# One planned TensorE stream of attention and feed-forward: new durations in the planner, new due times

## The chip, the cores and the metric

The kernel runs on one core of one Trainium2 chip. The metric is device microseconds of one execution. One more execution was recorded by the hardware profiler; all rows below come from it. The engines are TensorE (PE, with its weight loads as PEld), VectorE (DVE), ScalarE (ACT), GpSimd (POOL) and SyncE (SP), which issues the DMAs.

## The reference

Attention over 4 batches, 8 heads, 768 positions and head size 64, then a feed-forward network (FFN) over its 3072 tokens:

```
k_sum, v_sum = max of k, mean of v over blocks of 32 keys      # 24 of each
local  = q k^T / 8, only where |i - j| < 16
blocks = q k_sum^T / 8 + log(32)
a      = softmax over [local, blocks];  x = a @ [v, v_sum]      # 3072 x 512
out    = relu(x @ w_in)^2 @ w_out                               # 512 -> 2048 -> 512
```

## The kernel before, in words

**Tiling.** Attention works on 48 groups of 64 queries (12 to a batch), all 8 heads at once. For each group `softmax` masks and exponentiates (DVE L830, ACT L887) and normalises on DVE (L906) or, as a letter of `NORMAL_BY` says, on ACT (L913). `visit` multiplies with v for a pair of groups, and splits the 128 x 256 result x in two float32r parts, `xh` (ACT L1062) and `xl` (DVE L1065), from which the FFN reads. The block maxima of k come from `batch_k`: a DMA per head pair (`KL`), then DVE L566 (`KM`).

**Weights.** `w_in` and `w_out` are 16 items f each, converted by `convert` on ACT and DVE (L1131, L1137, L1145) into two float32r parts, which stay in SBUF.

**FFN.** Tokens are in 6 units of 512. Units 0 and 1 are plain: for each of 16 items f, `ffn` computes h = w_in^T x (task `FIu_f`, 12 matmuls, L1195), relu into `rl` (`RL`, ACT L1204), its square (`SQ`, L1205), a rounded copy `gh` (`GH`, L1206) and the rest `gl` (`GL`, DVE L1209), and then adds to the output in PSUM (`FOu_f`, L1219). There are two `h` tiles and one `rl` tile: `FI` of item f + 2 needs `RL` of item f done, and `RL` of item f + 1 needs `GL` of item f done. Items 0 and 1 of unit 0 run in halves of 256 tokens (`a`, `b`). `put` copies the outputs out of PSUM (L1256, `PC`) and stores them. Units 2 to 5 go as two couples through seven products of sums of blocks (`products`, `mixed`, L1514, L1731). For these `combine` (POOL L1300) and `combine_in` form sums of `w_out` and `w_in` for 8 pairs p of items, two halves each. `combine_in` adds the parts (`RCi`, L1364), sums blocks (`SCi`, L1379), and splits (ACT L1382, DVE L1385); a letter of `HALF_SUMS_BY` gives the sums of a pair to POOL or DVE. The result `ci` is stored to DRAM and read back later.

**What sets the order.** No instruction is placed by hand. Each piece of work is a `Task` with an engine, a modelled duration, a due time (`key`), tasks that it follows, and buffers that it takes or uses. `Plan.order()` simulates the five engines: whenever an engine is free it starts the ready task with the lowest due time whose buffers are free, and lets it last its modelled duration. The order of starts is the order in which the kernel's instructions are issued, one queue for each engine; at run time every engine works its queue strictly in that order and waits by semaphores. So a modelled duration costs the chip nothing: it only changes which task comes first. The due times are constants at the head of the file (`VISITS`: when each pair of groups is due; `SUMS`: each half of `combine_in`; `COMBS`: each `combine`; and so on). In the model a DVE task of a kind named in `SHARED`, started while POOL is busy, lasts longer by the factor `slows` of the POOL task times what it shares with it. Temporaries of 128 x 1024 float32 (weights in conversion, `cr`, `cs`, `ci`, output tiles `os`) take turns in three buffers `t`, in the order planned: a tile can start when the tile before it in its buffer is through, its store included.

Of the kernel before, what the change touches and what calls it, by code (L numbers as in the profile page):

```python
# [28 lines left out]
SQ = 32  # L29
# [25 lines left out]
FV_AT = 60.61, 233.96  # L55
# [130 lines left out]
class Plan:  # L186
# [26 lines left out]
    def order(self):  # L213
# [15 lines left out]
        for t in self.tasks:  # L229
# [3 lines left out]
            t.shared = t.engine == "DVE" and kind in self.SHARED  # L233
# [20 lines left out]
        while events:  # L254
# [25 lines left out]
            for e, tasks in ready.items():  # L280
# [46 lines left out]
def attention_then_relu2_ffn(  # L327
# [268 lines left out]
    def batch_v(b):  # L596
# [78 lines left out]
        if own:  # L675
# [4 lines left out]
            done(add(f"VM{b}", "PE", 1.4, sum_up, key + 8, [*all_loads, t_means], take=[out_ps], use=all_x))  # L680
# [92 lines left out]
    def window(g):  # L773
# [9 lines left out]
        return add(f"KW{g}", "ACT", 0.63, copy, wanted(g - 2) + 3, keys_of(g - 1, range(NPAIR))[1:], take=[x])  # L783
# [6 lines left out]
    def first_attention(g):  # L790
# [212 lines left out]
    def visit(both, then=(), block_sums=None):  # L1003
# [15 lines left out]
        if block_sums:  # L1019
# [6 lines left out]
            block_sums_done(add(f"VM{g}", "PE", 1.4, sum_up, due - 1, more, take=[out_ps], use=x))  # L1026
# [10 lines left out]
        def products():  # L1037
# [5 lines left out]
            f"V{both[-1]}" if n else f"S{then[0]}", "PE", 0.54 * n + 0.11 * (n == 1) + 0.49 * len(then), products, due, deps, take=take + [s] * bool(s), use=use,  # L1043
# [127 lines left out]
    def ffn(u, f, o, done, half=None):  # L1171
# [31 lines left out]
        t1 = t_FI[u, f] = add(f"FI{name}", "PE", 2.73 if half is None else 2.0, hidden, due, deps, take=[h], use=wi)  # L1203
        t2 = add(f"RL{name}", "ACT", act, lambda: nc.scalar.activation(cut(r), cut(h), AF.Relu), due + 3, [t1], take=[r], use=[h])  # L1204
# [782 lines left out]
```

## Time and profile before

| | us |
|---|---|
| median of 3 runs | 584.36 |
| lowest and highest run | 582.04, 586.36 |
| span of the profiled execution | 581.0 |
| TensorE busy in it | 563.0 (97%) |
| VectorE, ScalarE, GpSimd busy | 452.2, 373.7, 134.5 |

The profiled execution is known by its span alone: the lowest timed run is 1.04 us above it, the median 3.36, so what lies around the span is at least about that. Of the page's slices, TensorE shows 9 tenths in nearly all from the fourth on, with its clock at full speed; VectorE's busy share is highest in the first 16 of 40 slices (up to 230 us) and falls to half in the last third; the DMA engines are at 8 to 9 tenths up to slice 24 (350 us) and at 5 to 7 after it. The FFN's plain units and most of the attention lie before 300 us; the products of the two couples fill the rest. A row such as `[1.24 <-DMA scr_s<-cs]` says how long the engine stood idle before that instruction and which event ended it.

### The profile page before, as it was taken

The numbers are of one execution on the slowest core, as the hardware profiler recorded it, in microseconds if no ns is written. First come the engines' busy times: TensorE is split into PE (matmuls) and PEld (weight loads), VectorE is DVE, ScalarE is ACT, GpSimd is POOL, SyncE is SP. The second block draws the span as 40 slices with busy tenths as digits, with TensorE's granted clock in tenths as the row PEclk, the third lists the DMA queues.
The fourth block names the chain that finished last, engine by engine and source line by source line (L and its number), as shares of the span: only waits on it lengthen the run. The fifth ranks groups of instructions, "written<-read, shape, count | busy, mean of one in ns | idle before, by whom it ended". The sixth has DMA issues, their size and how long they took to land.

```text
span 581.0 us, 12047 instructions
## 1 busy us (share of the span) xinstructions
PE 563.0 (97%) x4052; PEld 460.2 (79%) x4052; DVE 452.2 (78%) x1015; ACT 373.7 (64%) x968; POOL 134.5 (23%) x193
## 2 busy tenths in 40 slices
PE   7879999999999899999999999999999999999997
PEld 6668787888887688887888888888888888888885
DVE  4899999685799997879976978869932656868864
ACT  1899899786757787768765768464634642454442
POOL 4300010167669469500043430000000000000000
PEclk9999999999999999999999999999999999999999
DMA  8899996989997999999988888866875566667672
GB/s 298 295 382 340 332 337 243 323 327 341 304 381 236 327 358 338 364 333 335 312 271 246 268 257 257 268 181 192 256 240 175 178 195 192 196 195 226 196 227 98
DMA packets 88082, 157.15 MB, mean 270 GB/s; under 512 B 9066, under 2 KB 30926, under 8 KB 88022
## 3 DMA queue, kind: packets, MB, share of 16 engines
q1 hardware_dynamic: 88022, 156.39, 82.2%
q8 instruction: 32, 0.52, 0.4%
q14 instruction: 28, 0.23, 0.1%
HBM read 111.30 MB, written 44.66 MB: 268 GB/s over the span
## 4 chain that ended last, share of the span: by engine, by line
PE 76%; DVE 9%; DMA 8%; SPq 3%; issue 2%; ACT 1%; DVEq 0%; ACTq 0%
PE o L1514 23%; PE o L1731 14%; PE h L1195 9%; PE o L1219 9%; PE sz L1731 8%; PE att L1514 4%; PE x L997 3%; DMA raw<-wW 3%; PE att L756 2%; PE sa L1731 2%; PE att L1731 2%; DMA v<-vS 1%; DMA fv_lent<-vS 1%; DMA out<-os 1%; DVE ci L1379 1%
## 5 line engine op out<-in xcount | busy, mean ns | idle before, releaser
L1496 ACT CAST gh<-g 128x512 fp32r<-128x512 f32 x112 | 69.3, 621 | 63.2 <-DVE gl L1501 30.5
L1514 PE MATMUL o<-gh,w 128*128 128x512 f32 x384 | 103.0, 390 | 0.0
L1501 DVE TENSOR_TENSOR gl<-g,gh 128x512 fp32r<-128x512 f32 x112 | 76.8, 693 | 22.9 <-ACT gh L1496 22.4
L1514 PEld LDWEIGHTS o<-gh,w 128*128 128x128 f32 x384 | 71.8, 188 | 15.0
L1195 PE MATMUL h<-xh,w 128*128 128x512 f32 x240 | 76.2, 399 | 3.9 <-ACT rl L1204 3.9
L1768 ACT ACTIVATE g<-g 128x512 f32<-128x512 f32 x60 | 37.6, 630 | 49.5 <-DVE g L1764 49.3
L887 ACT ACTIVATE p<-p,small 128x118 f32<-128x118 f32 x160 | 61.1, 387 | 1.6 <-DVE small L830 1.6
L1219 PE MATMUL o<-w,gh 128*128 128x512 f32 x240 | 61.9, 394 | 0.0
L1514 PE MATMUL o<-gl,w 128*128 128x512 f32 x192 | 59.2, 389 | 0.0
L1195 PEld LDWEIGHTS h<-xh,w 128*128 128x128 f32 x240 | 45.1, 191 | 14.2 <-ACT rl L1204 4.7
L1219 PEld LDWEIGHTS o<-w,gh 128*128 128x128 f32 x240 | 44.4, 188 | 9.7 <-issue 0.4
L1195 PE MATMUL h<-xl,w 128*128 128x512 f32 x120 | 47.2, 394 | 0.0
L1514 PEld LDWEIGHTS o<-gl,w 128*128 128x128 f32 x192 | 36.0, 188 | 7.6
L1731 PE MATMUL o<-w,w 128*128 128x512 f32 x160 | 40.6, 390 | 0.0
L769 POOL COPY kb<-kb 128x96 f32<-128x96 f32 x25 | 10.9, 435 | 107.1 <-PE att L756 36.4
L1774 POOL TENSOR_TENSOR g<-g 128x512 f32<-128x512 f32 x16 | 22.6, 1418 | 53.7 <-ACT g L1768 53.1
L1731 PEld LDWEIGHTS o<-w,w 128*128 128x128 f32 x160 | 30.0, 188 | 6.3
L1491 DVE TENSOR_TENSOR g<-g 128x512 f32<-128x512 f32 x48 | 33.9, 716 | 1.2 <-POOL g L1774 0.7
L830 DVE CUSTOM_DVE_ANT_0 p<-att,mask 128x118 f32<-128x118 f32 x152 | 32.5, 272 | 2.6 <-PE att L756 2.6
L1731 PE MATMUL sz<-xh,w 128*128 128x512 f32 x128 | 34.5, 391 | 0.0
L1219 PE MATMUL o<-w,gl 128*128 128x512 f32 x120 | 33.6, 389 | 0.0
L1764 DVE CUSTOM_DVE_ANT_0 g<-sz,g 128x512 f32<-128x512 f32 x32 | 21.9, 685 | 13.2 <-ACT g L1751 6.4
(201 smaller groups left out, 1186.7 us busy)
## 6 DMA issues: line engine op xcount, KB each, us to landing
raw<-wW SPq DMA_DIRECT2D x32, 512.0 KB
w<-scr_t SPq DMA_DIRECT2D x64, 256.0 KB
w<-scr_s SPq DMA_DIRECT2D x64, 256.0 KB
w<-scr_a SPq DMA_DIRECT2D x48, 256.0 KB
w<-scr_i SPq DMA_DIRECT2D x44, 256.0 KB
turn<-a SPq DMA_DIRECT2D x18, 512.0 KB
scr_t<-ci SPq DMA_DIRECT2D x16, 512.0 KB
v<-vS SPq DMA_DIRECT2D x34, 192.0 KB
```

The lines of the kernel that those rows point to most:

```text
L830: nc.vector.tensor_tensor_reduce(out=pr.tile[:, j, :KEYS], in0=score_at(g, 0, j), in1=mask_of(g)[0], scale=-SCALE, scalar=-NEG, op0=ALU.ad ...
L887: nc.scalar.activation(x, score_tile(g, p % parts)[:, p] if by_pe else x, AF.Exp, bias=nm.tile[:, p : p + 1], scale=SCALE if by_pe else -1 ...
L1195: nc.tensor.matmul(cut(h), lhsT=lhs.tile[:, k // 2, k % 2 * P : (k % 2 + 1) * P], rhs=rhs[:, k, c0 : c0 + n], start=(i == 0), stop=(i == 3 ...
L1219: nc.tensor.matmul(o_of(o, t).rearrange("p (h c) -> p h c", h=2), lhsT=terms[i][0].tile[:, (t - t0) * P : (t - t0 + 1) * P], rhs=terms[i][ ...
L1491: lambda x=x, ins=ins, op=op: nc.vector.tensor_tensor(out=x.tile, in0=ins[0].tile, in1=ins[1].tile, op=op),
L1496: f"GH{s}_{n}", "ACT", 0.54, lambda x=x, gh=gh: nc.scalar.copy(out=gh.tile, in_=x.tile), due - GH_LEAD, ready,
L1501: lambda x=x, gh=gh, gl=gl: nc.vector.tensor_tensor(out=gl.tile, in0=x.tile, in1=gh.tile.bitcast(F32), op=ALU.subtract),
L1514: nc.tensor.matmul(o.tile[:, d], lhsT=chunk.tile[:, w * HALF + d * P : w * HALF + (d + 1) * P], rhs=y.tile, start=begins and w == 0 and y ...
L1731: nc.tensor.matmul(o.tile, lhsT=lhs(w, k), rhs=y[k], start=begins and i == 0, stop=i == 5, skip_group_check=not begins,)
L1764: lambda: nc.vector._custom_dve(TENSOR_ADD_SAT, out=to.tile, in0=o.tile, in1=x.tile, s0=HUGE, s1=0.0), key, deps,
L1768: f"G{name}_{s}", "ACT", 0.63, lambda: nc.scalar.activation(to.tile, to.tile, AF.Square), key + 0.7, [t], use=[to]
L1774: f"{name}_{s}", engine, cost, lambda: tensor.tensor_tensor(out=to.tile, in0=a.tile, in1=b.tile, op=ALU.subtract), key, deps,
```

## The change

It changes what the planner believes, and the due times; the tasks are the same, but that one group's normalisation moves from DVE to ACT (one letter of `NORMAL_BY`). Modelled durations become shorter for most small tasks (L1256 and others 0.69 to 0.615, half an `FI` 2.0 to 1.47, scores 1.1 to 0.97). The cost of a switch of TensorE to narrow tasks goes from 0.3 to 0.09, with 0.13 for the way back. `t.shared`, true or false before, becomes a factor: 2.5 for `SCi`, 1.5 for `N`, 1.8 for `XPL`, 1.2 for `RCi`, 1 for the other shared kinds. The due times are set anew, most of them by under 8 us.

```diff
+VM0_AT = -60
-FIRST_LS = -180
+FIRST_LS = -160
...
-NORMAL_BY = "DDDDDDDDDDDDAADDDDDAADDADDAAAADDADDDDAADAAAAAAAA"
...
+NORMAL_BY = 'DDDDDDDDDDDDAADDDDDAADDADDAAAADDADADDAADAAAAAAAA'
...
-COMBS = 113.9, 126.8, 141.39, 159.1, 177.9, 210.24, 223.15, 214.82
...
+COMBS = (113.677, 126.8, 141.39, 159.1, 178.36, 210.24, 219.634, 214.224)
...
-R_LEAD = 9
-TR_LEAD = 16.82
...
-X_LEAD = 5.36
...
+R_LEAD = 12
+TR_LEAD = 9.85
...
+X_LEAD = 18.99
...
-    SWITCH, NEAR = 0.3, 9.0
+    SWITCH, BACK, NEAR = 0.09, 0.13, 9.0
     NARROW = ("S", "V", "VM")
-    SHARED = "GL", "TA", "TB", "WJ", "WW", "SL", "SLi", "XD", "XSL", "XPL", "XW", "RCi", "SCi", "N"
+    SHARED = "GL", "TA", "TB", "WJ", "WW", "SL", "SLi", "XD", "XSL", "XPL", "XW", "XPL", "RCi", "SCi", "N"
+    TWICE = dict(SCi=2.5, N=1.5, XPL=1.8, RCi=1.2)
...
-            t.shared = t.engine == "DVE" and kind in self.SHARED
+            t.shared = self.TWICE.get(kind, 1.0) * (t.engine == "DVE" and kind in self.SHARED)
...
-                        cost += slows * min(cost, free["POOL"] - now)
+                        cost += slows * t.shared * min(cost, free["POOL"] - now)
                 if e == "POOL":
                     slows = t.slows
-                free[e] = end = now + cost + self.SWITCH * (t.narrow and not narrow)
+                if e == "PE":
+                    cost += self.SWITCH * (t.narrow and not narrow) + self.BACK * (narrow and not t.narrow)
+                free[e] = end = now + cost
...
-    SUMS = 121.7, 129.74, 148.43, 166.33, 195.88, 201.13, 197.53, 197.25, 153.98, 169.96, 168.64, 165.29, 173.06, 198.45, 180.64, 190.85
...
+    SUMS = (121.7, 122.391, 148.43, 166.33, 197.9, 203.15, 204.48, 196.35, 156.0, 171.98, 168.64, 166.253, 173.06, 198.338, 180.64, 190.85)
...
-    A0, A1, B0, B1 = 12.0, 2.0, 21.0, 2.2
-    HALF_AT = 26.97, 32.0
+    T0, SLOW, STEP = 28.0, 6.4, 6.68
+    MIXED_STEP = (1.54, 1.47)
+    X_BY = (20.008, 15.505)
+    SUMS = (121.7, 122.391, 148.43, 166.33, 197.9, 203.15, 204.48, 196.35, 156.0, 171.98, 168.64, 166.253, 173.06, 198.338, 180.64, 190.85)
+    PRODUCT_STEP = (1.517, 1.34)
+    A0, A1, B0, B1 = 10.3, 1.69, 21.18, 1.77
+    HALF_AT = (26.97, 32.657)
...
-        t1 = t_FI[u, f] = add(f"FI{name}", "PE", 2.73 if half is None else 2.0, hidden, due, deps, take=[h], use=wi)
-        t2 = add(f"RL{name}", "ACT", act, lambda: nc.scalar.activation(cut(r), cut(h), AF.Relu), due + 3, [t1], take=[r], use=[h])
-        t3 = add(f"SQ{name}", "ACT", act, lambda: nc.scalar.activation(cut(r), cut(r), AF.Square), due + 4, [t2], use=[r])
+        t1 = t_FI[u, f] = add(f"FI{name}", "PE", 2.72 if half is None else 1.47, hidden, due, deps, take=[h], use=wi)
+        t2 = add(f"RL{name}", "ACT", act - 0.04, lambda: nc.scalar.activation(cut(r), cut(h), AF.Relu), due + 3, [t1], take=[r], use=[h])
+        t3 = add(f"SQ{name}", "ACT", act - 0.02, lambda: nc.scalar.activation(cut(r), cut(r), AF.Square), due + 4, [t2], use=[r])
```

Line numbers of the changed kernel are 1 higher from line 40 on, 2 from line 198 on and 4 from line 314 on.

**VectorE before the first halves of the FFN (about 35 to 42 us).** An `xl_75` is the rest of one group's x, the last of them that of group 7, which `FI0_0b` needs; `raw`, `t` and `w` are weights in conversion; `p0` and `small3` with L899, L900 and L906 the normalisation of group 8. Before:

```order
L1131 TENSOR_SCALAR raw1_1_486<-raw1_1_486 128x512
L1065 TENSOR_TENSOR xl_75<-att1_69,xh_74 128x4x64
L1137 SCALAR_TENSOR_TENSOR t1_1_663<-t1_1_663,raw1_1_486 128x512
L1145 TENSOR_TENSOR w1_0_711<-t1_0_660,w1_0_711 128x2x256
L1131 TENSOR_SCALAR raw0_2_492<-raw0_2_492 128x512
L1131 TENSOR_SCALAR raw3_516<-raw3_516 128x1024
L899 TENSOR_SCALAR small3_88<-small3_88 128x4
L900 RECIPROCAL small3_88<-small3_88 128x4
L1145 TENSOR_TENSOR w1_1_730<-t1_1_663,w1_1_730 128x2x256
L1065 TENSOR_TENSOR xl_75<-att0_68,xh_74 128x4x64
L906 TENSOR_TENSOR p0_82<-p0_82,small3_88 128x4x118
L1065 TENSOR_TENSOR xl_75<-att1_69,xh_74 128x4x64
```

And with the change, `gl0_0a` being the first `gl` of the FFN:

```order
L1149 TENSOR_TENSOR w1_0_713<-t1_0_679,w1_0_713 128x2x256
L1141 SCALAR_TENSOR_TENSOR t1_1_739<-t1_1_739,raw1_1_490 128x512
L1069 TENSOR_TENSOR xl_75<-att1_69,xh_74 128x4x64
L1135 TENSOR_SCALAR raw0_2_501<-raw0_2_501 128x512
L903 TENSOR_SCALAR small3_88<-small3_88 128x4
L904 RECIPROCAL small3_88<-small3_88 128x4
...
L910 TENSOR_TENSOR p0_82<-p0_82,small3_88 128x4x118
L1149 TENSOR_TENSOR w1_1_753<-t1_1_739,w1_1_753 128x2x256
L1213 TENSOR_TENSOR gl0_0a_780<-rl0_0a_751,gh0_0a_777 128x256
```

Two L1131 (of `raw0_2` and `raw3`), the normalisation of group 8 and the last step of `w1_1` (L1145) stood ahead of the last `xl`; they now stand behind it (`raw3` further on). The work ahead of `gl0_0a` is nearly the same.

**VectorE in the middle (about 160 to 180 us).** `ci4_0` is the first half of the sums of `w_in` pair 4, `kb` the block maxima of a new batch, `gl1_2` to `gl1_4` the FFN's unit 1. Before:

```order
L1385 TENSOR_TENSOR ci1_0_2113<-ci1_0_2113 128x4x128
L1209 TENSOR_TENSOR gl1_2_2245<-rl1_2_2207,gh1_2_2238 128x512
L566 TENSOR_REDUCE kb_73<-kb_73 128x24 x3
L1209 TENSOR_TENSOR gl1_3_2280<-rl1_3_2248,gh1_3_2277 128x512
L1364 TENSOR_TENSOR ci4_0_2286<-w8_1133 128x2x128
L1364 TENSOR_TENSOR ci4_0_2286<-w9_1179 128x2x128
L1379 TENSOR_TENSOR ci4_0_2286<-ci4_0_2286 128x128 x4
L1385 TENSOR_TENSOR ci4_0_2286<-ci4_0_2286 128x4x128
L1209 TENSOR_TENSOR gl1_4_2353<-rl1_4_2288,gh1_4_2351 128x512
```

And with the change:

```order
L1213 TENSOR_TENSOR gl1_2_2236<-rl1_2_2176,gh1_2_2214 128x512
L1368 TENSOR_TENSOR ci4_0_2242<-w8_1174 128x2x128
L1368 TENSOR_TENSOR ci4_0_2242<-w9_1332 128x2x128
L1383 TENSOR_TENSOR ci4_0_2242<-ci4_0_2242 128x128 x4
L570 TENSOR_REDUCE kb_73<-kb_73 128x24 x2
L1389 TENSOR_TENSOR ci1_0_2234<-ci1_0_2234 128x4x128
L1213 TENSOR_TENSOR gl1_3_2303<-rl1_3_2244,gh1_3_2277 128x512
L1389 TENSOR_TENSOR ci4_0_2242<-ci4_0_2242 128x4x128
L1213 TENSOR_TENSOR gl1_4_2353<-rl1_4_2311,gh1_4_2350 128x512
```

The sums of `ci4_0` (two L1364, four L1379) stood behind `gl1_3`; they now stand ahead of two `kb`, of `ci1_0` and of `gl1_3`.

**ScalarE ahead of the relu of item 6 (about 176 to 185 us).** `xh` is the split of a pair's x, `kw29` the keys of group 29, `p0` and `p1` softmax of groups 26 and 27. Before:

```order
L1382 CAST ci5_1_2355<-ci5_1_2355 128x4x128
L1205 ACTIVATE rl1_5_2373<-rl1_5_2373 128x512
L1206 CAST gh1_5_2450<-rl1_5_2373 128x512
L1382 CAST ci1_1_2420<-ci1_1_2420 128x4x128
L1204 ACTIVATE rl1_6_2505<-h1_6_2404 128x512
L1062 CAST xh_74<-x23_2461 128x4x128
L1205 ACTIVATE rl1_6_2505<-rl1_6_2505 128x512
```

And with the change:

```order
L1210 CAST gh1_5_2467<-rl1_5_2355 128x512
L1386 CAST ci5_1_2357<-ci5_1_2357 128x4x128
L1066 CAST xh_74<-x23_2433 128x4x128
L891 ACTIVATE p0_82,small3_88<-p0_82,small3_88 128x118 x2
L1386 CAST ci1_1_2385<-ci1_1_2385 128x4x128
L891 ACTIVATE p0_82,small3_88<-p0_82,small3_88 128x118 x2
L891 ACTIVATE p1_83,small1_72<-p1_83,small1_72 128x118 x4
L917 ACTIVATE p0_82<-p0_82,small3_88 128x118 x4
L784 COPY kw29_2562<-kb_73 128x4x24
L785 COPY kw29_2562<-kb_73 128x4x94
L917 ACTIVATE p1_83<-p1_83,small1_72 128x118 x4
L1386 CAST ci5_0_2503<-ci5_0_2503 128x4x128
L1208 ACTIVATE rl1_6_2586<-h1_6_2401 128x512
L1209 ACTIVATE rl1_6_2586<-rl1_6_2586 128x512
```

The relu of item 6 stood ahead of the split for pair 23, of the keys and of two groups' exponentials and normalisations, and now stands behind them.

## Rows read from the trace of the kernel before

**Rows 1.** The page: its head, and busy time of the engines.
```profile
span 581.0 us, 12047 instructions
...
PE 563.0 (97%) x4052; PEld 460.2 (79%) x4052; DVE 452.2 (78%) x1015; ACT 373.7 (64%) x968; POOL 134.5 (23%) x193
```

**Rows 2.** Waits of TensorE: us in total, times, longest us.
```profile
PE h L1195 <- ACT rl L1204: 3.9, 3, 2.7
...
PE o L1731 <- DVE g L1764: 0.3, 1, 0.3
```

**Rows 3.** TensorE's timeline: start us, us, instruction, idle before it with releaser.
```profile
41.03 0.50 PE L1195 MATMUL h_0b<-xh,w 128*128 128x256 f32 x2 [1.65 <-ACT xh L1062]
...
69.79 0.73 PE L1195 MATMUL h<-xh,w 128*128 128x512 f32 x2 [0.81 <-ACT rl L1204]
```

**Rows 4.** VectorE's timeline before 42 us.
```profile
27.86 0.44 DVE L1131 TENSOR_SCALAR raw<-raw 128x512 uint32<-128x512 uint32 x1 [1.01 <-DMA raw<-wW]
...
38.67 1.02 DVE L1131 TENSOR_SCALAR raw<-raw 128x512 uint32<-128x512 uint32 x2
...
41.44 0.41 DVE L1065 TENSOR_TENSOR xl<-att,xh 128x256 fp32r<-128x256 f32 x1
```

**Rows 5.** TensorE's timeline at 201 us.
```profile
201.23 1.22 PE L1195 MATMUL h<-xh,w 128*128 128x512 f32 x2 [2.72 <-ACT rl L1204]
```

**Rows 6.** The chain of waits in order of time: start us, us, what.
```profile
201.23 4.55 PE h L1195 x12
...
208.51 2.72 PE h L1195 x12
```

**Rows 7.** Stretches: PE, PEld, DVE, ACT, POOL busy, PEclk, DMA share, GB/s.
```profile
42.00:44.00 2.00, 1.99 (x15) 1.79 (x16) 2.00 (x10) 2.00 (x5) 0.00 (x0) 1.00 1.03 327
...
180.00:190.00 10.00, 9.63 (x97) 7.76 (x95) 9.64 (x28) 5.97 (x21) 9.77 (x13) 1.00 0.60 206
...
200.00:205.00 5.00, 3.77 (x10) 3.02 (x11) 5.00 (x23) 4.89 (x16) 2.87 (x4) 0.66 1.07 382
...
210.00:215.00 5.00, 5.00 (x54) 3.91 (x54) 4.74 (x8) 2.61 (x5) 3.51 (x5) 1.00 1.06 411
```

**Rows 8.** VectorE's timeline from 157 to 200 us.
```profile
157.66 0.69 DVE L1256 COPY os<-o 128x512 f32<-128x512 f32 x1 [1.24 <-DMA scr_s<-cs]
...
161.66 0.68 DVE L1209 TENSOR_TENSOR gl<-rl,gh 128x512 fp32r<-128x512 f32 x1
...
162.26 2.67 DVE L566 TENSOR_REDUCE kb<-kb 128x24 f32<-128x768 f32 x3
...
166.50 1.78 DVE L1364 TENSOR_TENSOR ci<-w 128x256 f32<-128x256 f32 x2 [0.53 <-DMA out<-os]
...
168.31 2.92 DVE L1379 TENSOR_TENSOR ci<-ci 128x128 f32<-128x128 f32 x4
...
196.08 1.01 DVE L1379 TENSOR_TENSOR ci<-ci 128x128 f32<-128x128 f32 x4
...
197.64 0.71 DVE L1364 TENSOR_TENSOR ci<-w 128x256 f32<-128x256 f32 x2
...
199.81 0.68 DVE L1209 TENSOR_TENSOR gl<-rl,gh 128x512 fp32r<-128x512 f32 x1
```

**Rows 9.** GpSimd's timeline.
```profile
164.12 1.30 POOL L1300 TENSOR_TENSOR cr<-w 128x512 f32<-128x512 f32 x1 [7.24 <-PE o L1219]
```

**Rows 10.** The chain of waits: two landings.
```profile
160.64 5.74 DMA out<-os
...
256.12 4.87 DMA kb<-kT
```

**Rows 11.** ScalarE's timeline.
```profile
166.01 0.60 ACT L1204 ACTIVATE rl<-h 128x512 f32<-128x512 f32 x1 [0.36 <-DVE gl L1209]
...
184.64 0.60 ACT L1204 ACTIVATE rl<-h 128x512 f32<-128x512 f32 x1 [3.95 <-DVE gl L1209]
```

**Rows 12.** TensorE's timeline at 169 us.
```profile
169.41 0.63 PE L756 MATMUL att<-kb,q 64*64 64x118 f32 x16
```

More of the change, by code (lines that the diff above doesn't have):

```diff
@@ L654, in batch_v @@
             last = add(
-                f"VM{b}_{i}", "PE", 0.9, mm, key + i, loads + [t_means, last],
+                f"VM{b}_{i}", "PE", 0.98, mm, VM0_AT + i, loads + [t_means, last],
                 take=[out_ps] if i == 0 else [], use=[x] + [out_ps] * (i > 0),
@@ L781, in copy @@
             nc.scalar.copy(out=x.tile[:, :, NB:], in_=kb[:, :, k0 + NB : k0 + KEYS])
-        return add(f"KW{g}", "ACT", 0.63, copy, wanted(g - 2) + 3, keys_of(g - 1, range(NPAIR))[1:], take=[x])
+        return add(f"KW{g}", "ACT", 0.59, copy, wanted(g - 2) + 3, keys_of(g - 1, range(NPAIR))[1:], take=[x])
     def keys_of(g, pairs):
@@ L1024, in sum_up @@
                     mm()
-            block_sums_done(add(f"VM{g}", "PE", 1.4, sum_up, due - 1, more, take=[out_ps], use=x))
+            block_sums_done(add(f"VM{g}", "PE", 1.44, sum_up, due - 1, more, take=[out_ps], use=x))
         if then:
@@ L1042, in visit @@
         t_v = add(
-            f"V{both[-1]}" if n else f"S{then[0]}", "PE", 0.54 * n + 0.11 * (n == 1) + 0.49 * len(then), products, due, deps, take=take + [s] * bool(s), use=use,
+            f"V{both[-1]}" if n else f"S{then[0]}", "PE", 0.535 * n + 0.08 * (n == 1) + 0.485 * len(then), products, due, deps, take=take + [s] * bool(s), use=use,
         )
@@ L1534, in products @@
                 made["U1"] = add(
-                    f"U1_{s}", "ACT", 0.97, lambda o=o: nc.scalar.copy(out=by_two(u2), in_=o.tile), due, [t_p], take=[u2], use=[o]
+                    f"U1_{s}", "ACT", 0.92, lambda o=o: nc.scalar.copy(out=by_two(u2), in_=o.tile), due, [t_p], take=[u2], use=[o]
                 )
@@ L1603, in split @@
             t1 = add(
-                f"XSH{s}_{i}_{k}", "ACT", 0.62, lambda: nc.scalar.copy(out=hi[k].tile, in_=temps[i][k].tile), due + key,
+                f"XSH{s}_{i}_{k}", "ACT", 0.53, lambda: nc.scalar.copy(out=hi[k].tile, in_=temps[i][k].tile), due + key,
                 [*t_x[i, k], *needs, *t_X[s][at][:1], *(x_readers[0][at] if s else [])], take=take, use=[both[i]] + [hi[k]] * (not take),
@@ L1622, in sum_x @@
                 t = add(
-                    f"XW{s}_{i}_{k}", "DVE", 0.69, whole, due - XS_LEAD + i + 0.1 * k, [t_XL[g] for g in range(u * UG, (u + 1) * UG)],
+                    f"XW{s}_{i}_{k}", "DVE", 0.615, whole, due - XS_LEAD + i + 0.1 * k, [t_XL[g] for g in range(u * UG, (u + 1) * UG)],
                     take=[] if k else [both[i]], use=[both[i]] * k, behind=t if k else None, keeps=not k, begin=due - XS_LEAD - 4,
@@ L1634, in plainly @@
             t1 = add(
-                f"XPH{s}_{i}_{k}", "ACT", 0.62, lambda: nc.scalar.copy(out=hi, in_=temps[i][k].tile), due + key - 2, [*t_x[i, k], *deps],
+                f"XPH{s}_{i}_{k}", "ACT", 0.53, lambda: nc.scalar.copy(out=hi, in_=temps[i][k].tile), due + key - 2, [*t_x[i, k], *deps],
                 use=[both[i]],
@@ L1750, in evacuate @@
             return add(
-                f"{name}_{s}", "ACT", 0.59, lambda: nc.scalar.copy(out=to.tile, in_=o.tile), key, deps, take=take, use=[o] + [to] * (not take)
+                f"{name}_{s}", "ACT", 0.52, lambda: nc.scalar.copy(out=to.tile, in_=o.tile), key, deps, take=take, use=[o] + [to] * (not take)
             )
@@ L1755, in plus @@
             return add(
-                f"{name}_{s}", "DVE", 0.69, lambda: nc.vector.tensor_tensor(out=to.tile, in0=o.tile, in1=x.tile, op=ALU.add), key, deps,
+                f"{name}_{s}", "DVE", 0.615, lambda: nc.vector.tensor_tensor(out=to.tile, in0=o.tile, in1=x.tile, op=ALU.add), key, deps,
                 use=[o, x, to],
@@ L1831, in step @@
                         t = add(
-                            f"R21_{p}_{s}", "ACT", 0.6, lambda: nc.scalar.activation(second.tile, x.tile, AF.Relu), key, [t],
+                            f"R21_{p}_{s}", "ACT", 0.52, lambda: nc.scalar.activation(second.tile, x.tile, AF.Relu), key, [t],
                             use=[second, x],
@@ L1835, in step @@
                         t_G[s, p, 1] = add(
[L1836 removed]
+                            f"G21_{p}_{s}", "ACT", 0.57, lambda: nc.scalar.activation(second.tile, second.tile, AF.Square), key + 0.7,
                             [t], use=[second],
```

57 lines of the change are left out of this document (26 added, 31 removed).

## The prediction, before the changed kernel was run

> **What bounds the kernel now.** I read the page first: TensorE is busy 563.0 of 581.0 us [rows 1], so all that an order of work can win are 18.0 us, the start and the end of the program among them. No other engine is near that. The table of TensorE's waits comes next: where does it wait after the start? The relu is the releaser with the largest sum for the hidden products, 3.9 us in three waits, the longest 2.7 [rows 2]. So I went to TensorE's timeline for the places. There are two stretches.
>
> At the front, `FI0_0b`, the second half of the first hidden product, waits 1.65 us at 41.03, and `FI0_6` waits 0.81 for a relu at 69.79 [rows 3]. The first row names ScalarE's `xh`; VectorE's timeline shows the last `xl` at 41.44 [rows 4], so the splits of x as a whole are late there, and VectorE makes the last of them.
>
> In the middle, `FI1_9` waits 2.72 us at 201.23 [rows 5]. The chain of waits shows that this costs twice: its twelve matmuls take 4.55 us, where the next twelve take 2.72 [rows 6]. The stretch of 200 to 205 us has a mean granted clock of 0.66, so TensorE was for a part at 1.2 instead of 2.4 GHz [rows 7]. The loss is 4.55 − 2.72 = 1.83 us beside the 2.72 of the wait. After the wait of 1.65 us at 41.03 the granted clock was 1.00 [rows 3, 7]: a wait of that length cost no clock there.
>
> What is late at 201.23? The relu of item 8 needs the one `rl` tile back, and `gl1_7` on VectorE gives it at 199.81 + 0.68 [rows 8]. From 157 us on VectorE hardly stands still, so the sum of its work before `gl1_7` is what sets the time of that wait.
>
> **The change part by part.** The modelled durations, the switch costs and the factors cost the chip nothing: they only choose the order. TensorE, VectorE, ScalarE and GpSimd do the same work but for one normalisation that goes from VectorE to ScalarE after the two stretches; I cost it at nothing, since neither engine has TensorE waiting on it there, and if that cover went it would cost one VectorE instruction, below 1 us.
>
> *Front.* Between the start of the two L1131 at 38.67 and the last `xl` at 41.44 there are 2.77 us; less one other `xl` (0.41, as the row at 41.44) it is 2.36 us of work that now stands behind the last split [rows 4]. That is more than the 1.65 us which TensorE waited, so this wait should go. Against it, `gl0_0a`, which the next products need, keeps nearly its place; VectorE's idle time of 1.01 us at 27.86 [rows 4], before a weight that is waited for, can be filled by the new order and would bring `gl0_0a` forward by as much. So the gain lies between 0 and 1.65; I take 1.2, between the 1.01 that VectorE can give and the whole. The wait of 0.81 at 69.79 goes if two pieces of other TensorE work come between, as the new order of TensorE has it (the fourth output product and a visit): between 0 and 0.81, taken 0.8. Front: **2.0**, bounds 0 and 2.46.
>
> *Middle.* Three changes move `gl1_7`. (a) VectorE's idle 1.24 us at 157.66, before an output copy that waited for a buffer [rows 8], goes, since this copy now follows other work: 1.24 earlier. (b) The sums of `ci4_0` stood at 166.50 to 171.2, beside GpSimd, which is at work from 164.12 on after 7.24 us idle [rows 9]. They took 1.78 + 2.92 us there; the same two groups take 0.71 and 1.01 at 197.64 and 196.08 [rows 8]. Moved ahead, they save between 0 (beside GpSimd again) and 2.98 us. I take 1.7: `gl1_2` starts at 161.66 [rows 8], so that the sums come up to 3 us before GpSimd's start, but (c) they need a buffer whose output tile must first be stored. Before, such a store went from 160.64 for 5.74 us to 166.38 [rows 10], and the sums stood 0.53 waiting for it [rows 8]. In the new order the tile in question is an earlier one. The wait lies between 0 and 166.38 − 162.3 = 4.1; I take 1.9, rather below the middle because its stores now go out ahead of two loads of keys. So `gl1_7` comes 1.24 + 1.7 − 1.9 = 1.0 us earlier. The wait at 201.23 shrinks from 2.72 to 1.7, which is nearest to the row at 41.03 (1.65, no clock lost), so the 1.83 stay as well. Middle: 1.0 + 1.83 = **2.8**, bounds 0 and 2.72 + 1.83 = 4.55.
>
> *ScalarE's queue.* The relu of item 6 now stands behind a split, keys, eight exponentials and two normalisations. I cost this at nothing because ScalarE stood idle 3.95 us before it, waiting for VectorE [rows 11]: the work fits where the engine was idle. If that cover is gone, each us that the relu comes later is one of wait for `FI1_8`.
>
> *The queue of SyncE.* Stores and loads change places, among them the two loads of keys named above; what this may cost is the second rival. The rest of the program, from 300 us on, has VectorE at half load, and I found no wait of TensorE there that the new order touches.
>
> Sum: 2.0 + 2.8 = 4.8 us, so the span goes from 581.0 to 576.2. The profiled execution lies 3.36 us below the median and 1.04 below the fastest run; I take the saving off the median: 584.36 − 4.8 = **579.6**. One per cent is 5.8 us here, about what a measurement of this kernel tells from no change: faster begins below 578.5, slower above 590.2.
>
> **The rivals.**
>
> *B: the middle's gain is taken back by the DMA.* From 200 to 205 us the DMA engines are busy at a share of 1.07; room is only before, 10 × (1 − 0.60) = 4.0 us from 180 to 190 [rows 7]. The keys of the last batch land at 256.12 + 4.87 = 261.0 [rows 10], and their maxima let a sum start for which TensorE waits 0.3 us [rows 2]: there is no slack. If that landing stays where it is, a TensorE that arrives there 2.8 us sooner waits 2.8 us more. For it: no transfer up to there becomes smaller. Against it: the 4.0 us can be filled when the issues come sooner. Time: 584.36 − 2.0 = 582.4. A rule speaks for this rival: the Trainium skill, "SBUF — State Buffer", section "A bandwidth-pool intuition that's wrong (but worth ruling out)", gives HBM to one core some 358 GB/s and says that HBM is almost always the bottleneck. Here 382 GB/s were moved from 200 to 205 us and 411 from 210 to 215 [rows 7], above that figure, so the trace bears out that the stretch is full but not where the limit lies.
>
> *C: everything goes.* The three waits on a relu (3.9 [rows 2], with the 0.81 and the 2.72 among them), the 1.65 and the 1.83: 7.4 us, 577.0. For it: (c) is short if the store lands early, and then (b) gives its 2.98; `gl1_7` comes 4.2 earlier. Against it: the 1.9 above.
>
> *D: slower, by the buffer of `ci4_0`.* If the sums are held as long as before, to 166.4, VectorE stands idle from about 161.1 (162.3 less the 1.24) and then runs them beside GpSimd all the same: 166.4 + 4.70 = 171.1. Behind them wait two of the block maxima (2 × 0.89), one split (0.7) and `gl1_3` (0.7 [rows 8]), which ends near 174.3 instead of 166.0. The relu of item 4, which waited 0.36 for it at 166.01 [rows 11], ends near 174.9, and the visit that starts at 169.41 [rows 12] needs its `h` tile: TensorE waits 5.5 us and loses the clock (1.83, as at 201.23). It decides from the point where `gl1_3` is 169.41 − 166.6 = 2.8 us late; from there each us costs one. What comes back: the visit's delay takes up most of the wait at 201.23 and its clock, 3.9 of 4.55. With the front's 2.0 this gives 5.5 + 1.83 − 3.9 − 2.0 = 1.4 us more: 585.8, and beyond 590.2 where a second relu is late behind it, another 2.72 + 1.83 at item 6. For it: the buffers are three, and the landing of 5.74 us is in the trace. Against it: another tile's store, issued sooner.
>
> *E: the change doesn't do what it says.* The new order is different in places that TensorE doesn't feel: 584.4.
>
> **How the numbers follow.** The forecast has 0.47; its own range is 577 to 582, from the bounds of front and middle, and 0.4 of it lie below 578.5. B has 0.15, C 0.19, D 0.14 (half of it beyond 590.2), E 0.05. Faster: 0.47 × 0.4 + 0.19 = 0.38. Slower: 0.07. Within: 0.55. The range reaches from 575.0, two us under C, to 587.0, a little over the first case of D; what is left out is D's dearer half and a tail of C, about 0.1.
>
> **What would show it.** In the profile after: no wait of 1.65 us at `FI0_0b`, and VectorE's last `xl` near 39 us; no wait before the seventh item's hidden product; the `ci4_0` sums at 0.7 and 1.0 us rather than 1.78 and 2.92, with the idle time before them naming the store; the wait of `FI1_9` under 2 us with the clock at 1.00. I am wrong if the sums are again near 4.7 us, if another relu than item 8's stops TensorE between 165 and 200 us, or if the wait at the last keys grows beyond 0.3.

## The result, and the profile after

The change made the kernel slower. Beside the kernel before on the same chip its median was 587.74 us against 584.36 (7 runs each), a ratio of 1.0055 (95% interval 1.0034 to 1.0075); in a later series it was 586.81 against 584.62, 1.0039 (1.0008 to 1.0069). Both intervals lie above 1: the loss is small, but clear of noise. The forecast was 579.6, with a range of 575.0 to 587.0.

The profiled execution has a span of 586.0 us, 5.0 more than before [rows 1]; the medians lie 3.4 us apart, and a second profile of the changed kernel has a span of 582.1. What follows is read from the first one. The page's head and busy times:

```profile
span 586.0 us, 12045 instructions
...
PE 564.3 (96%) x4052; PEld 461.6 (79%) x4052; DVE 455.2 (78%) x1014; ACT 376.3 (64%) x972; POOL 133.2 (23%) x193
```

TensorE is busy 1.3 us longer, so 3.7 of the 5.0 us are idle. The table of TensorE's waits (us in total, times, longest) shows that the place that leads it is new:

```profile
PE o L1735 <- ACT os L1260: 4.1, 1, 4.1
```

Here are these places on TensorE's timeline (start, us, instruction, idle before it with its releaser). They answer to [rows 3, 5, 12]:

```profile
40.27 0.50 PE L1199 MATMUL h_0b<-xh,w 128*128 128x256 f32 x2 [0.27 <-ACT rl_0a L1208]
...
43.13 0.50 PE L1199 MATMUL h_1b<-xh,w 128*128 128x256 f32 x2 [1.18 <-ACT rl_1a L1208]
...
171.59 1.15 PE L1001 MATMUL x<-a,v 118*64 118x64 f32 x32 [1.70 <-ACT rl L1208]
...
201.12 1.22 PE L1199 MATMUL h<-xh,w 128*128 128x512 f32 x2 [2.08 <-ACT rl L1208]
...
261.52 1.48 PE L1735 MATMUL o<-xh,w 128*128 128x512 f32 x4 [4.13 <-ACT os L1260]
```

The wait of 1.65 us at `FI0_0b` is gone (0.27 left), and 1.18 stands in its place at `FI0_1b`. The visit at 171.6 waits 1.70 us, which it didn't before. `FI1_9` waits 2.08 instead of 2.72. And at 261.52 the sum `SP0_2` waits 4.13; before the change it began without a wait:

```profile
257.53 1.20 PE L1731 MATMUL o<-xh,w 128*128 128x512 f32 x4
```

If one sets the end of each TensorE task beside its end before, the course of the whole is seen: 0.24 us ahead at 50 us (`FI0_2`), 1.03 ahead at 81 (`FO0_5`), 0.65 ahead at 169 (`FO1_1`), 1.18 behind at 176 (`FO1_2`), 0.18 ahead again at 257 (`VM3`), 5.63 behind at 267.5 (`SP0_4`) and 4.78 behind at the end. So in this pair of executions the loss, 4.98 us from 0.18 ahead to 4.80 behind, arises between 257 and 301 us: 4.13 of wait and 1.7 of clock behind it (8 us at 0.79, where it was 1.00 before), less 0.8 that comes back, 0.29 of it the wait that the kernel before has at 263.55. The stretches (columns as in [rows 7]), two of the changed kernel and then one of the kernel before:

```profile
200.00:205.00 5.00, 3.88 (x11) 3.07 (x12) 5.00 (x22) 4.75 (x17) 3.85 (x6) 0.66 1.03 340
...
262.00:270.00 8.00, 8.00 (x30) 6.38 (x29) 6.58 (x10) 3.99 (x10) 0.00 (x0) 0.79 1.01 366
```

```profile
262.00:270.00 8.00, 7.71 (x88) 5.69 (x86) 8.00 (x15) 6.44 (x14) 0.27 (x1) 1.00 1.05 380
```

At 201 us the clock falls as before (0.66 in both [rows 7]).

What ended the wait at 261.52 is read from VectorE's timeline, from SyncE's and from the chain of waits. VectorE first:

```profile
254.47 0.64 DVE L910 TENSOR_TENSOR p<-p,small 128x472 f32<-128x472 f32 x1
258.96 0.69 DVE L1260 COPY os<-o 128x512 f32<-128x512 f32 x1 [3.85 <-DMA scr_s<-cr]
...
260.20 0.65 DVE L1260 COPY os<-o 128x512 f32<-128x512 f32 x1
```

`SP0_2` needs the PSUM tile that the last two of unit 1's four output copies empty: `PC1_2` (VectorE, 260.20) and behind it `PC1_3` (ScalarE, 260.88 in the chain below), which is the `os` that the row at 261.52 names. `PC1_2` stands on VectorE behind `PC1_0` (L1260, 258.96), and that one could have gone at 255.1 and waited 3.85 us for a DMA, a store of `cr`. Each of the two copies takes a `t` buffer. There are nine of them by then, not three, since six buffers of converted weights join them; the plan gives the copies the two that the stores of `combine`'s pair 6 (`WS6_0` of `cr`, `WS6_1` of `cs`) hold until they land. SyncE's issues in the changed kernel:

```profile
244.12 2.87 SPq L638 DMA_DIRECT2D fv<-vS  x4
247.04 2.82 SPq L979 DMA_DIRECT2D a<-turn  x4
250.25 0.35 SPq L701 DMA_DIRECT2D q<-qW  x1
251.47 0.33 SPq L712 DMA_DIRECT2D v<-vS  x1
252.50 0.35 SPq L701 DMA_DIRECT2D q<-qW  x1
253.66 0.32 SPq L712 DMA_DIRECT2D v<-vS  x1
254.07 0.39 SPq L1328 DMA_DIRECT2D scr_s<-cr  x1
254.66 1.46 SPq L1328 DMA_DIRECT2D scr_s<-cs  x1
```

and in the kernel before:

```profile
247.03 0.49 SPq L1324 DMA_DIRECT2D scr_s<-cr  x1
247.62 0.51 SPq L1324 DMA_DIRECT2D scr_s<-cs  x1
248.22 1.45 SPq L697 DMA_DIRECT2D q<-qW  x1
```

Before, the two stores went out at 247.03 and 247.62, directly behind the last load of `fv`. Now four reads (L979) and four loads of q and v stand ahead of them, and the stores go out at 254.07 and 254.66. What most of these eight wait for is not their own data. This program's DMAs use eight semaphores in turn, and an issue goes out only when the transfer eight issues before it has landed: of SyncE's waits for a landing 92 of 96 in the kernel before and 76 of 83 in the changed one are of this kind. So each issue ahead of a store can cost it the landing of an older transfer, and these were slow: the last load of `fv` took 7.09 us, at a DMA share of 0.99 from 246 to 265 us. The chain of waits (start, us, what) has the rest:

```profile
246.50 7.09 DMA fv<-vS
...
253.66 0.32 SPq L712
...
254.07 4.80 DMA scr_s<-cr
...
258.96 0.69 DVE os L1260
...
260.20 0.66 DVE os L1260
...
260.88 0.59 ACT os L1260
...
261.52 4.62 PE o L1735 x12
```

The store takes 4.80 us to land, and the copy `PC1_0` starts 0.09 us later. TensorE's 4.62 us for twelve matmuls (2.72 at full clock [rows 6]) include the lower clock.

Why did the planner put the stores there? In its own account of time the two stores become ready at 237.9 and 238.5 (their splits end at 235.3 and 235.9, and it adds 2.6 us). At 238.39 SyncE comes free and starts the load `QL37`; it and three more loads, each with a lower due time than the stores (200 to 212 against 229), follow one another at 0.5 us each. In the plan of the kernel before, the buffer of `QL37` came free only at 241.76, behind the stores at 240.17 and 240.86. On the planner's SyncE none of the loads waits, and there is no limit of eight. On the chip the two loads of q waited 1.0 and the two of v 1.5 us for landings of `fv`.

### The profile page after: what moved, and what is told of

Read it like the earlier page. It is cut to its first block, busy times and chain, and to the rows that moved or that the text cites. A ratio compares the mean times of both kernels' runs of the same rounds, so it can differ in the third digit from the quotient of the medians.

```text
span 586.0 us, 12045 instructions
## 1 busy us (share of the span) xinstructions
PE 564.3 (96%) x4052; PEld 461.6 (79%) x4052; DVE 455.2 (78%) x1014; ACT 376.3 (64%) x972; POOL 133.2 (23%) x193
## 4 chain that ended last, share of the span: by engine, by line
PE 71%; DMA 13%; DVE 6%; ACT 6%; SPq 2%; issue 1%; DVEq 0%; ACTq 0%
PE o L1518 22%; PE o L1735 14%; PE sz L1735 8%; PE h L1199 7%; PE o L1223 7%; PE att L1518 4%; PE x L1001 3%; PE sa L1735 2%; DMA raw<-wW 2%; PE att L760 2%; PE att L1735 2%; DMA scr_s<-cr 2%; ACT p L891 1%; DMA fv<-vS 1%; DMA scr_a<-w 1%
## 5 line engine op out<-in xcount | busy, mean ns | idle before, releaser
L1735 PE MATMUL o<-xh,w 128*128 128x512 f32 x112 | 31.2, 402 | 4.1 <-ACT os L1260 4.1
L1213 DVE TENSOR_TENSOR gl<-rl,gh 128x512 fp32r<-128x512 f32 x30 | 24.5, 817 | 11.2 <-ACT gh L1210 11.1
```

Source lines behind the costliest of these rows:

```text
L1213: lambda: nc.vector.tensor_tensor(out=cut(gl), in0=cut(r), in1=cut(gh).bitcast(F32), op=ALU.subtract),
L1735: nc.tensor.matmul(o.tile, lhsT=lhs(w, k), rhs=y[k], start=begins and i == 0, stop=i == 5, skip_group_check=not begins,)
```

## The experiments

Each kernel takes the order that the planner gives and moves single tasks ahead of others in it; the work stays the same. The moves are pairs (task, the task that it goes ahead of):

```
planned = plan.order()
for name, ahead_of in MOVES:
    t, x = (next(y for y in planned if y.name == n) for n in (name, ahead_of))
    planned.remove(t)
    planned.insert(planned.index(x), t)
```

Two kernels take parts of the change instead. Ratios are to the kernel before on the same chip.

**The stores first, in the changed kernel.**

```diff
+MOVES = ("WS6_0", "TR33_0"), ("WS6_1", "TR33_0")
```

> The changed kernel with the two stores of combine's pair 6 (WS6_0, WS6_1) moved on SyncE's queue ahead of four reads and four loads (TR33, QL37, LV32, QL38, LV33); nothing else moves. Theory 1 (a store behind waiting loads on SyncE keeps the t buffer that the output copy at 259 us needs): the stores go out near 247 us, land near 252, the copy is not held, TensorE's wait of 4.13 us at 261.5 and the 0.83 us of low clock behind it go: 587.7 - 4.96 = 582.8. Theory 2 (the copy is late because the DMA engines are full there, whatever the order): the wait stays, 587.7. Theory 3 (the time is lost in many small places): within 1 us of 587.7.

Measured: ratio 0.9991 (0.9967 to 1.0016), against 1.0055 and 1.0039 for the change. The wait at 261.5 is nearly gone; another has come behind it:

```profile
257.68 1.21 PE L1740 MATMUL o<-xh,w 128*128 128x512 f32 x4 [0.18 <-ACT os L1265]
...
265.42 1.51 PE L1740 MATMUL o<-xh,w 128*128 128x512 f32 x4 [1.97 <-DVE g L1773]
```

The stores go out at 247.77 and 248.24 now. So the order on SyncE caused the wait (theory 1), and it accounts for the change's loss within the intervals. The time came down to 584.2, not to 582.8. The wait of 1.97 us belongs to the keys of the last batch, which went out after the stores and all loads, the first of them at 256.63.

**The stores last, in the kernel before.**

```diff
+MOVES = ("WS6_0", "KL3_0"), ("WS6_1", "KL3_0")
```

> The kernel before with the same two stores moved back on SyncE's queue, to just ahead of the four loads of keys (KL3), where the change puts them. Theory 1: they go out near 255 us instead of 247, land near 260, the output copy starts near 260 instead of 255.3, TensorE waits some 4 to 5 us before the sum SP0_2 and loses up to 0.8 of clock: 584.4 + 5 = 589.4, which is slower than the changed kernel. Theory 2: unchanged, 584.4.

Measured: 1.0026 (1.0000 to 1.0053). The profile has the wait in the forecast size at the forecast place:

```profile
200.92 0.73 PE L1200 MATMUL h<-xh,w 128*128 128x512 f32 x2 [2.71 <-ACT rl L1209]
...
259.93 1.22 PE L1736 MATMUL o<-xh,w 128*128 128x512 f32 x4 [4.05 <-ACT os L1261]
```

but the median rose by about 1.5 us, not 5. So the order alone makes the wait in the kernel before, too, and costs less there than the wait is long. Its profiled execution shows one part of the reason: the clock after the wait of 2.71 at 200.92 was 1.00, where the kernel before shows 0.66, so it came to 257 us earlier. Whether that is so in most executions is open.

**gl of item 7 earlier.**

```diff
+MOVES = ("SQ1_7", "SH4_1"), ("GH1_7", "SH4_1"), ("GL1_7", "RCi7_0_1")
```

> The changed kernel with gl of item 7 in unit 1 moved ahead of three groups on VectorE (the second L1368 of ci7_0, the split of ci6_0, the sums of ci7_0), and its square and rounding ahead of two splits on ScalarE. It should come near 197.6 us instead of 199.7, so the relu of item 8 near 198.4 instead of 200.5 and TensorE's wait of 2.08 us at 201.1 with its 1.83 us of low clock go. Theory 1a (SyncE's loads before 254 us are set by landings, not by TensorE, so the held copy stays where it is): TensorE only waits 3.9 us longer at 261.5, 587.7. Theory 1b (SyncE's queue moves along with TensorE): 587.7 - 3.9 = 583.8. Rival: the splits and sums that are put back 0.7 us stop TensorE elsewhere: above 587.7.

Measured: 1.0065 (1.0035 to 1.0095), no better than the change. The wait at `FI1_9` should have gone and is still 1.41 us, and the one before `SP0_2` is 4.74: the 0.67 us won at the first are nearly all (0.61) waited for at the second, as theory 1a has it. The next kernels show that the first wait had a second cause, too.

**gl of item 3 earlier.**

```diff
+MOVES = ("GL1_3", "KM2_2"),
```

> The changed kernel with gl of item 3 in unit 1 moved on VectorE ahead of two block maxima and one split (2.7 us). The relu of item 4 then comes near 168 instead of 170.9 us and the wait of 1.70 us of the visit at 171.6 goes. Theory A (VectorE's whole work up to gl of item 7 sets when item 9 can start): TensorE waits those 1.7 us longer at 201.1, 587.7. Theory B (each wait counts by itself): 587.7 - 1.7 - 0.2 = 585.8.

Measured: 1.0028 (1.0005 to 1.0052). The visit's x no longer waits, but its scores wait 0.93 and 0.44 us for the block maxima that were put back, and `FI1_9` still waits 1.83. The intervals overlap with the change's; the two theories are not told apart.

**Stores and keys first.**

```diff
 MOVES = ("WS6_0", "TR33_0"), ("WS6_1", "TR33_0"),
+    ("KL3_0", "TR33_0"), ("KL3_1", "TR33_0"), ("KL3_2", "TR33_0"), ("KL3_3", "TR33_0")
```

> The changed kernel with the two stores of pair 6 and also the four loads of the last batch's keys (KL3) ahead of TR33, QL37, LV32, QL38 and LV33 on SyncE. With the stores alone a wait of 1.97 us was left at 265.4, on VectorE's first sum behind the maxima of these keys, with the mean clock at 0.79 from 262 to 270. Theory 1 (order on SyncE): the keys go out near 250 instead of 256.6 us, land near 257, that wait and its clock go: ratio to the kernel before 0.995 (581.5 to 582). Theory 2 (the DMA engines are full there, so a load that goes out sooner lands no sooner): the keys land near 261 as before, or the stores do: ratio 0.999 as with the stores alone.

Measured: 0.9966 (0.9942 to 0.9991), the first that beats the kernel before. The keys go out from 248.40, no wait of TensorE for them is left, and the clock is 1.00 from 250 to 275 us. `SP0_2` waits a little again:

```profile
257.12 1.21 PE L1744 MATMUL o<-xh,w 128*128 128x512 f32 x4 [1.20 <-ACT os L1269]
```

That is not for a later copy: `PC1_2` began at 255.79, where it began at 256.35 with the stores alone. But TensorE came 1.6 us sooner, since its clock did not fall at 201 us in this execution (1.00 from 200 to 205 us, 0.66 there). Of the two theories each holds a part. The third of the four loads of keys went out at 251.33 instead of 257.69 and landed at 259.14 instead of 263.79: of the 6.4 us that the order on SyncE won, 1.7 were lost in a longer transfer, at a DMA share of 1.03 from 246 to 258 us.

**The same, with both gl earlier.**

```diff
+    ("SQ1_7", "SH4_1"), ("GH1_7", "SH4_1"), ("GL1_7", "RCi7_0_1"), ("GL1_3", "SLi1_0")
```

> The same, and gl of item 7 ahead of three groups on VectorE with its square and rounding ahead of two splits on ScalarE, and gl of item 3 ahead of one split on VectorE. If the queue on SyncE was what gave the earlier gain back, the waits at 171 (1.3 to 1.7) and 201 us (1.8 to 2.1, in some executions with 1.8 of clock) now count: ratio 0.995 - 0.006 = 0.989 (578.5). If TensorE only arrives sooner at landings that don't move: ratio as without them, 0.995, with a wait of 2 to 4 us between 255 and 268.

Measured: 0.9953 (0.9929 to 0.9977), 582.75 us against 585.54, the lowest ratio of all. The gain over the kernel above is within the noise and far from 0.989. The wait at 171 us is gone, but `FI1_9` waits 2.62 although its `gl1_7` came at 197.67. ScalarE's timeline shows why:

```profile
201.03 0.62 ACT L1399 CAST ci<-ci 128x512 fp32r<-128x512 f32 x1 [2.35 <-DVE ci L1396]
201.56 0.59 ACT L1221 ACTIVATE rl<-h 128x512 f32<-128x512 f32 x1
```

The relu (L1221) at 201.56 stood behind the split of `ci7_0` (L1399), which waited 2.35 us for VectorE's sums, those that I had put back. One queue's cure was the next queue's block.

**The model alone, a part of the due times alone.** The first keeps the change's durations and factors and takes all due times, leads and the letter of `NORMAL_BY` from before. The second is not its reverse. It has the old durations (but for one small `VM` task) and, of the new due times, only those at the head of the file; `SUMS`, `HALF_AT`, `X_BY`, the steps and the other constants inside the function are the old ones. So it mixes two sets of due times, although its expectation speaks of the new ones as a whole, and the new due times with the old durations were not run.

> The changed planner durations, switch costs and factors with the due times, leads and the normalisation letter of before (VM0_AT apart, which is left out). In this order the two stores of pair 6 stand behind the four loads of keys too. Theory 1: they go out near 258 us or later, the output copy is held 2 to 3 us longer than with the whole change: a wait of 6 to 8 us before the sum SP0_2, 591 or more (ratio 1.011 or more). Theory that the new durations are the good part of the change: faster than before, ratio below 0.998.

> The new due times, leads and the normalisation letter with the planner's old durations, switch costs and factors. Here the two stores stand directly behind the last loads of FV3, ahead of all reads and loads. Theory 1: no wait of over 1 us before the sum SP0_2. The time as a whole hangs on other queues that fall as they may: 584 to 590; the theory that the due times are the good part: ratio below 0.998.

Measured: 1.0149 (1.0102 to 1.0196) for the model alone, 1.0102 (1.0069 to 1.0135) for the part of the due times. The first shows that the new durations do harm with the old due times. What the whole set of new due times does by itself stays open. Both lose most at the same sum `SP0_2`:

```profile
268.34 2.07 PE L1734 MATMUL o<-xh,w 128*128 128x512 f32 x4 [10.70 <-ACT os L1259]
```

```profile
263.43 2.07 PE L1732 MATMUL o<-xh,w 128*128 128x512 f32 x4 [6.61 <-ACT os L1257]
```

For the model alone that is as expected in kind, and larger (6 to 8 us were forecast): the stores stand behind the keys and go out at 258.94. For the part of the due times my expectation was a miss: the stores went out at 246.45 and the first copy was in time, but the second copy stood on VectorE behind three block maxima whose keys landed late. The chain of waits of that kernel:

```profile
256.56 5.49 DMA kb<-kT
...
262.07 0.69 DVE os L1257
...
263.43 5.49 PE o L1732 x12
```

**The part of the due times, the copy first.**

```diff
+MOVES = ("PC1_2", "KM3_0"),
```

> The new due times with the old durations (measured at 1.0102 of the kernel before), and the second output copy of unit 1 on VectorE (PC1_2) ahead of the three block maxima of the last keys, behind which it stood there. In that run TensorE waited 6.61 us at 263.4; the copy stood behind maxima whose keys landed at 262. If this order on VectorE is the cause: the copy near 257.5, the wait 0 to 2 us, ratio 1.002. If the stores or the DMA engines are: the wait stays over 5 us, ratio 1.010.

Measured: 1.0044 (1.0024 to 1.0064), 0.6% less. The wait fell from 6.61 to 1.79 us; 1.84 came back as three waits for the maxima (0.35, 0.54, 0.95). The order on VectorE was the cause there.

**The whole chain of item 7 first; the front.**

```diff
+    ("GL1_6", "RCi6_0_0"), ("RL1_7", "RCi6_0_1"), ("SQ1_7", "RCi6_0_1"), ("GH1_7", "RCi6_0_1"),
+    ("GL1_7", "RCi6_0_1"), ("RL1_8", "SH4_1")
...
+    ("WR1_1", "WJ0_1"), ("E8_2", "WH1_1"), ("E8_3", "WH1_1"), ("GL0_0a", "E9_0"), ("RL0_1a", "E9_0"),
+    ("WM0_2", "E9_0"), ("WH1_1", "E9_0"), ("WW1_1", "WJ0_2"), ("N8", "WJ0_2")
```

Both kernels keep the stores, the keys and `GL1_3` of the fastest one. The first two lines stand in place of its three moves for item 7; the second kernel has the other two lines as well.

> The stores and keys first on SyncE, gl of item 3 ahead of one split, and now item 7's whole chain in front: gl of item 6 ahead of the sums of ci6_0 and ci4_1 on VectorE; relu, square and rounding of item 7 ahead of the splits that wait for these sums on ScalarE; gl of item 7 ahead of the second L1368 of ci6_0; relu of item 8 ahead of the splits of cs4 and of the ci6_0 and ci7_0 that wait for sums. In the run before, gl of item 7 alone came forward and TensorE still waited 2.62 us at 202, since the relu of item 8 stood on ScalarE behind the split of ci7_0, which waited 2.35 us for VectorE's sums. Theory Q (it is the order on ScalarE's queue): the relu of item 8 comes near 197, no wait near 200, ratio 0.9953 - 0.0045 = 0.991. Rival (VectorE's whole work sets the time, the sums put back stop TensorE later): a wait of 1 us or more between 195 and 250, ratio 0.995.

> The same, and at the front one L1135 (of raw1_1, whose load lands late) behind the normalisation of group 7, the first gl ahead of group 8's normalisation, and the relu of item 1's first half ahead of two weight steps on ScalarE. If VectorE's queue is what TensorE waits for there: the wait at 34 us shrinks by 1 us or more and the wait of 1.0 us at h_1b (43 us) goes: 2 us less than without, ratio 0.9875. If the loads that land before 45 us set the pace: ratio 0.991, with other waits in their place.

Measured: 0.9980 (0.9958 to 1.0002) and 0.9989 (0.9969 to 1.0010). Both miss theory Q's numbers. The profile of the second, whose execution was the longest of its twelve, shows the middle without any wait from 112 to 211 us, and where it went:

```profile
211.88 0.73 PE L1224 MATMUL h<-xh,w 128*128 128x512 f32 x2 [2.16 <-ACT rl L1233]
...
294.22 1.16 PE L1760 MATMUL o<-xh,w 128*128 128x512 f32 x4 [2.23 <-DMA w<-scr_i]
```

At 211.88 a later relu is late; VectorE, which frees its `rl`, stood still for only 0.52 us from 205 to 226 us, so what was put back is done there. At 294.22 TensorE waits 2.23 us for a load of weights, and `SP0_2` waits 1.12 again. This fits the rival, that VectorE's whole work and the landings set these times; no run takes work from VectorE to test it. At the front the waits at 34 us went as meant, but 0.89 and 0.33 came back at 43 to 45.

**The changed kernel again.**

> The changed kernel once more, on this chip, beside the kernels of this call: 1.0055 of the kernel before (1.003 to 1.008), with a wait of 3 to 5 us before the sum SP0_2 near 261 us.

Measured: 1.0039 (1.0008 to 1.0069), with 3.79 us of wait before `SP0_2`. The wait is there in each of its two profiles.

## Why the prediction was wrong

*What bounds the kernel.* Right: TensorE's waits, with the clock behind them, are all that an order can win or lose. But I read the waits that the kernel before had, and priced the change by them. The loss came at a place without a row in that table: `SP0_2` had no wait, and how much room it had I didn't ask.

*The queue of SyncE: the step that failed.* The prediction said that stores and loads change places and costed that at nothing, with a rival B for the keys alone. It named neither the two stores of pair 6 nor the eight issues that now stand ahead of them, nor the copy and the sum that wait behind. Measured: 4.13 us of wait and 1.7 of clock, 0.8 of which came back; undone, the ratio falls from 1.0055 to 0.9991. The numbers were at hand in the trace of the kernel before:

```profile
255.27 0.65 DVE L1256 COPY os<-o 128x512 f32<-128x512 f32 x1
...
256.17 0.69 DVE L1256 COPY os<-o 128x512 f32<-128x512 f32 x1 [0.25 <-PE o L1219]
```

The stores went out at 247.03 and 247.62 and landed at 253.06 and 254.44, and the copies that took their buffers began at 255.27 and 256.17. So there were 2.2 and 1.7 us of room for stores that moved back by 7. Rival B had the stretch right: with the stores first, it is its keys that cost 1.97 us. The Trainium skill says in "SBUF — State Buffer", section "A bandwidth-pool intuition that's wrong (but worth ruling out)", that HBM is almost always the bottleneck. These runs show only that the DMA engines were full there (share 0.99 from 246 to 265 us) and that a load sent sooner took longer (7.8 us instead of 6.1 for the third load of keys); they don't show whether HBM sets the limit.

*The gains.* They failed, too. Of the 4.8 us forecast, TensorE was 0.18 ahead at 257 us, just before that wait. And with the stores undone the ratio is 0.9991 (0.9967 to 1.0016), a gain of 0.5 us with an interval around nothing. The two terms follow.

*Front.* The sum's term was 2.0; measured are 0.24 us at 50 us and 1.03 at 81. The 1.65 us before `FI0_0b` went, as forecast, and the 0.81 at `FI0_6` went (the 0.8 were right). Of these 1.03 us, 0.65 were left at 169. What failed is the 1.2: `gl0_0a` came no earlier (42.18 against 41.78), and `FI0_1b` waited 1.18 us for the relu behind it. The objection stood in the text and was given too little weight.

*Middle.* The term was 2.8; measured is a loss of 1.8 at 171 us and a gain of 0.7 at 201, with 0.6 won between them (the 0.37 at 185 are gone). The parts, on VectorE's timeline:

```profile
157.94 0.69 DVE L1260 COPY os<-o 128x512 f32<-128x512 f32 x1 [2.24 <-PE h L1199]
...
163.51 1.30 DVE L1368 TENSOR_TENSOR ci<-w 128x256 f32<-128x256 f32 x2 [1.37 <-DMA out<-os]
164.85 1.91 DVE L1383 TENSOR_TENSOR ci<-ci 128x128 f32<-128x128 f32 x4
...
168.41 1.31 DVE L1389 TENSOR_TENSOR ci<-ci 128x512 fp32r<-128x512 f32 x1
169.64 1.21 DVE L1213 TENSOR_TENSOR gl<-rl,gh 128x512 fp32r<-128x512 f32 x1
...
199.69 0.69 DVE L1213 TENSOR_TENSOR gl<-rl,gh 128x512 fp32r<-128x512 f32 x1
```

(a) The idle 1.24 us before the copy should go and grew to 2.24; its releaser is now TensorE. (b) The sums took 1.30 + 1.91 instead of 4.70: 1.5 saved where 1.7 were forecast, but by luck. They were to come before GpSimd's start, and GpSimd now started sooner, ahead of them:

```profile
162.87 1.66 POOL L1368 TENSOR_TENSOR ci<-w 128x256 f32<-128x256 f32 x2 [11.59 <-DMA scr_s<-cs]
```

So they ran beside it all the same, and part of the saving was given back behind them: the next two splits (L1389) took 1.31 and 1.21 us beside GpSimd, where one took 0.69 at 161.05 in the kernel before, with GpSimd idle. (c) The buffer cost 1.37 where 1.9 were forecast; the forecast took off the whole 1.9, though 0.53 of such a wait stood in the kernel before already [rows 8]. In all `gl1_7` came at 199.69 instead of 199.81: 0.12 earlier, not 1.0. And what D described took place, in small: `gl1_3` ended at 170.85 instead of 165.98, the relu of item 4 came at 170.94, and the visit waited 1.70 us. D put the end of `gl1_3` at 174.3 and the price at 5.5. This relu is also the sign that the prediction named for being wrong: another than item 8's stopped TensorE between 165 and 200 us.

*ScalarE's queue.* Costed at nothing, and right: the relu of item 6 stopped TensorE nowhere.

*The clock.* A wait of 1.7 us should have kept the clock, after the row at 41.03. The wait became 2.08 and the clock fell to 0.66 again. The rule itself doesn't stand (below).

*The chances.* Slower by over 1% had 0.07, within 1% 0.55, and within it was. But the forecast's sign was wrong, and a loss of 3.4 us lay outside the range. Nor is one per cent what a measurement of this kernel tells from no change: the interval of the first comparison is 0.2% to either side.

## What to carry to other kernels

When an order is made anew, read not only the queues of the engines that wait now: for each store that frees a buffer, look up who takes the buffer next, and how much room lies between the store's landing and that use. On a queue that is worked in order, an issue that can wait must not stand ahead of a store that is ready. With a set number of transfers under way (eight here, by the program's semaphores), any issue behind slow transfers can wait, and a planner without that limit does not see it. And due times that were found with other durations are not neutral: the old ones with the new durations cost 1.5% in the one kernel that had them.

## What the runs showed of the hardware

The length of a wait did not tell whether TensorE's clock would fall. The changed kernel has two profiles. At the same place, `FI1_9`, TensorE waited 2.08 us in one and 2.06 in the other; behind it the mean granted clock from 198 to 210 us was 0.86 in the first (for a part at 1.2 instead of 2.4 GHz) and 1.00 in the second:

```profile
198.00:210.00 12.00, 9.92 (x65) 8.09 (x66) 11.86 (x36) 8.88 (x31) 8.51 (x14) 0.86 1.03 367
```

```profile
198.00:210.00 12.00, 11.22 (x52) 9.05 (x56) 11.86 (x36) 11.08 (x37) 9.74 (x16) 1.00 1.02 372
```

Over other kernels it was 1.00 after a wait of 2.71 us at this place (stores last, the first row) and 0.86 after 1.78 (stores first, the second):

```profile
198.00:210.00 12.00, 9.29 (x48) 7.61 (x45) 11.66 (x42) 10.88 (x37) 4.23 (x6) 1.00 0.95 320
```

```profile
198.00:210.00 12.00, 10.22 (x76) 8.25 (x69) 11.38 (x38) 9.16 (x31) 7.88 (x13) 0.86 0.99 355
```

A fall cost up to 1.8 us here, as much as several of the edits did, and the runs of one kernel spread over 6.9 us (581.44 to 588.3 in 35 runs of the kernel before). What decides whether the clock falls, these runs don't show.
